# First three of eight early chunks: the current token's weights from turned keys and receptances by the tensor engine, and the weighted values added through the unit matrix

## The chip, the cores and the metric

The kernel runs on one core of one Trainium2 chip. The core has a tensor engine (PE, which writes to the accumulator memory PSUM), a vector engine (DVE), a scalar engine (ACT), a general engine (POOL) and a sync engine (SP), which here only issues transfers. The engines run their own instruction streams and meet at semaphores. The metric is device microseconds of one execution, a median of several runs; lower is better.

## What is computed

Two stages. The first is a linear recurrence over time with a bonus for the current token (4 batches, 8 heads, 768 steps, 48 numbers a head):

```python
for t in range(S):
    kt, vt, rt = (k[:, :, t], v[:, :, t], r[:, :, t])
    cur = np.einsum('bhd,bhe->bhde', u[None] * kt, vt)
    y[:, :, t] = np.einsum('bhd,bhde->bhe', rt, state + cur)
    state = w[None, :, :, None] * state + np.einsum('bhd,bhe->bhde', kt, vt)
```

The second takes y as 3072 rows of 384 numbers: `h = x @ w_in; g = h * np.cos(h); return g @ w_out`, with 2048 columns in the middle. So the current token enters y with the weight a = sum over d of r·u·k (per token and head), times v; earlier tokens enter with powers of w.

## The kernel before

The recurrence is cut into chunks of 128 tokens of one batch. The first eight (EARLY = 8; chunks 0 to 3 are the first 128 tokens of the four batches, 4 to 7 the second) go the way shown below; the rest goes in half chunks of two batches. The second stage runs in six blocks of four chunks. One unit of it, h, is nine matmuls of 512 columns (L509; high and low parts of x and of w_in), followed on DVE and ACT by the cosine and the split of g into high and low parts, and later by nine matmuls with w_out (L522). A block can begin when its four chunks have their x, so chunks 0 to 3 feed the first unit and chunks 4 to 7 the third.

An early chunk takes these steps (helper `chunk`, L956 ff.): load r, k, v (SP); turn r and k (L1001, PE) and multiply them by tables of powers of w on the way out of PSUM (rT L1010, kT L1029, or the copy L1043 when k was decayed before it was turned); multiply kT and rT into scores, A (L1093, PE); m = r·k (L1016), times u (L1050), summed over each head's 48 numbers to `a` (L1057); write `a` on the diagonal of A by eight ACT instructions of one head each (L1066) or by two wide ones (L1072); copy the scores above the diagonal over it under a mask (L1101, two per chunk, DVE); x = v times A (L1128, PE), from chunk 4 on also the state part (L1115); the state z = k times v (L1162); x in high and low parts (xh L1183, xl L1192). The weights are turned into high and low parts of another format on the way (`conv`, L884 to L925; its last step for w_in is w_in_lo, L916).

Before the chunks, w is loaded and turned (L682), raised to powers (L689 to L699) and spread into the tables decT_r and decT_k (L722, L731); u is loaded to 32 partitions (L665) and copied to the other 96 (L674).

What sets the order: every step is an `op` with an engine, a cost, what it comes after and the buffers it takes. `Plan.one_pass` goes through them and on each engine picks, among those ready within a hold, the one with the lowest due time. The due times (DUES), holds (HOLDS) and second choices of engine (ALTS) are tables of numbers, one entry per op. PE gets short matmuls of zeros (L1758) where the planner sees it idle before the second stage. Buffers are rings: three k, three v, two r, six f, four half chunks of A, seven PSUM banks for the early chunks. A buffer is loaded anew when its last reader is done.

Of the kernel before, what the change touches and what calls it, by code (L numbers as in the profile page):

```python
# [9 lines left out]
F32 = mybir.dt.float32  # L10
F32R = mybir.dt.float32r
BF16 = mybir.dt.bfloat16
I32 = mybir.dt.int32
# [24 lines left out]
RAW_K = 2  # L38
EARLY = 8

DUES = (
# [398 lines left out]
def kernel(  # L440
# [34 lines left out]
    G = 32  # L475
# [1437 lines left out]
```

## Time and profile before

| | us |
|---|---|
| median of 3 runs | 483.97 (483.74 to 484.13) |
| the profiled execution | 484.58 |
| its span, first to last instruction | 482.9 |
| PE busy in the span | 472.4 |
| DVE, ACT, POOL busy | 365.4, 297.9, 212.1 |

The span is what the trace covers; 484.58 is the same execution's own time. In the trace a matmul in 32 bits shows two records, a transposing one a single record, so 8 matmuls of the program are 16 records. A record's end is modelled, and it overlaps the next record's start by about a tenth of a microsecond; from start to start is what a group costs. In the order printed below a row is the program's instruction.

### The profile page before, as it was taken

To read this page: it belongs to the slowest core of one execution; us is meant where nothing else is said; L and a number is where in the kernel's file an instruction comes from. 1 tells how busy PE (TensorE), PEld (TensorE's weight loads), DVE (VectorE), ACT (ScalarE), POOL (GpSimd) and SP (SyncE) were. 2 spreads that over 40 slices of the span, in tenths; PEclk is the share of its full clock that TensorE was granted. 3 is DMA by queue.
4 is the path that set the end of the run, shared out by engine and by line. 5 is a ranking of instruction groups with operands and counts; after the bars stand their busy time and mean duration, and the time that the engine had idled before them with its cause. 6 is when DMAs were issued, how large, how long until landed. Compare 5 with 4: busy or idle time off the path is not lost.

```text
span 482.9 us, 11764 instructions
## 1 busy us (share of the span) xinstructions
PE 472.4 (98%) x4480; PEld 391.5 (81%) x4480; DVE 365.4 (76%) x681; ACT 297.9 (62%) x661; POOL 212.1 (44%) x215
## 2 busy tenths in 40 slices
PE   8999999999999999999999999999999999999995
PEld 7777788788888888888888888888888888899994
DVE  7999898998998886768776876775895755744453
ACT  5988897877885555466655655655655544444342
POOL 6775438445536965546735515635534600000000
PEclk9999999999999999999999999999999999999998
DMA  7883456337258636387527636636565600010001
GB/s 151 178 204 98 128 139 167 100 103 187 76 139 173 123 70 138 84 203 158 157 63 196 158 90 126 149 99 142 164 144 137 181 24 1 25 42 2 1 1 69
DMA packets 139281, 55.39 MB, mean 115 GB/s; under 512 B 122164, under 2 KB 135124, under 8 KB 139220
## 3 DMA queue, kind: packets, MB, share of 16 engines
q1 hardware_dynamic: 139012, 54.45, 46.1%
q8 instruction: 36, 0.59, 0.5%
q14 instruction: 25, 0.20, 0.1%
q10 hardware_dynamic: 208, 0.15, 0.1%
HBM read 49.86 MB, written 4.72 MB: 113 GB/s over the span
## 4 chain that ended last, share of the span: by engine, by line
PE 88%; DVE 5%; ACT 3%; issue 1%; DMA 1%; POOL 0%; ACTq 0%; DVEq 0%; POOLq 0%
PE bank L509 39%; PE bank L522 34%; PE bank L515 7%; PE bank L1400 4%; PE bank L1480 3%; ACT A L1066 1%; DVE A L1101 1%; DVE k L1021 1%; PE bank L1093 1%; DVE f L892 1%; DMA ztu<-in_u_dram 1%; DVE w_in_lo L916 1%; DVE f L530 0%; DVE a L1057 0%; PE bank L1128 0%
## 5 line engine op out<-in xcount | busy, mean ns | idle before, releaser
L527 ACT ACTIVATE qi<-bank 128x512 int32<-128x512 f32 (+1 forms) x102 | 58.1, 573 | 103.6 <-PE bank L509 98.8
L530 DVE SCALAR_TENSOR_TENSOR f<-bank,qi 128x512 f32<-128x512 f32 (+1 forms) x102 | 66.4, 655 | 66.1 <-ACT qi L527 65.4
L509 PE MATMUL bank<-xh,w_in_hi 128*128 128x512 f32 x288 | 113.2, 393 | 0.3 <-DVE gl L1610 0.3
L509 PE MATMUL bank<-xh,w_in_lo 128*128 128x512 f32 x288 | 112.7, 391 | 0.5 <-DVE w_in_lo L916 0.5
L509 PE MATMUL bank<-xl,w_in_hi 128*128 128x512 f32 x288 | 112.3, 390 | 0.0
L522 PE MATMUL bank<-gh,w_out_hi 128*128 128x512 f32 x240 | 95.8, 399 | 0.0
L522 PE MATMUL bank<-gh,w_out_lo 128*128 128x512 f32 x240 | 93.5, 390 | 0.0
L522 PE MATMUL bank<-gl,w_out_hi 128*128 128x512 f32 x240 | 93.5, 390 | 0.0
L1610 DVE TENSOR_TENSOR gl<-bank,gh 128x512 fp32r<-128x512 f32 x94 | 64.1, 682 | 14.8 <-ACT gh L1607 13.4
L1604 DVE TENSOR_TENSOR bank<-bank,f 128x512 f32<-128x512 f32 x94 | 64.8, 692 | 11.3 <-ACT f L533 11.0
L533 ACT ACTIVATE f<-f 128x512 f32<-128x512 f32 (+1 forms) x102 | 61.2, 607 | 19.5 <-DVE f L530 19.0
L1607 ACT CAST gh<-bank 128x512 fp32r<-128x512 f32 x94 | 55.0, 585 | 28.6 <-PE bank L522 25.1
L509 PEld LDWEIGHTS bank<-xh,w_in_lo 128*128 128x128 f32 x288 | 54.1, 188 | 12.9 <-DVE w_in_lo L916 1.3
L1347 POOL TENSOR_TENSOR A<-rT,decT_r 48x512 f32<-48x512 f32 x32 | 41.5, 1296 | 50.7 <-PE bank L1480 41.9
L509 PEld LDWEIGHTS bank<-xh,w_in_hi 128*128 128x128 f32 x288 | 54.0, 188 | 11.9 <-DVE gl L1610 0.7
L509 PEld LDWEIGHTS bank<-xl,w_in_hi 128*128 128x128 f32 x288 | 54.1, 188 | 10.9
L522 PEld LDWEIGHTS bank<-gh,w_out_hi 128*128 128x128 f32 x240 | 45.0, 188 | 9.9
L522 PEld LDWEIGHTS bank<-gh,w_out_lo 128*128 128x128 f32 x240 | 45.0, 188 | 9.6
L522 PEld LDWEIGHTS bank<-gl,w_out_hi 128*128 128x128 f32 x240 | 45.1, 188 | 8.9 <-DVE gl L1610 0.3
L913 POOL TENSOR_TENSOR f<-f,raw 128x384 int32<-128x384 int32 x24 | 26.1, 1086 | 37.1 <-DVE f L904 14.4
L1381 POOL TENSOR_TENSOR A<-ident,a 64x512 f32<-64x512 f32 x32 | 34.3, 1073 | 17.1 <-DVE a L1373 15.8
L1342 POOL TENSOR_TENSOR kT<-kT,decT_k 112x512 f32<-112x512 f32 x16 | 20.9, 1306 | 27.4 <-DVE kT L1327 26.2
(144 smaller groups left out, 719.1 us busy)
## 6 DMA issues: line engine op xcount, KB each, us to landing
raw<-in_moe_w_in_dram SPq DMA_DIRECT2D x32, 384.0 KB
raw<-in_moe_w_out_dram SPq DMA_DIRECT2D x32, 384.0 KB
raw<-in_k_dram SPq DMA_DIRECT2D x63, 80.0 KB
raw<-in_r_dram SPq DMA_DIRECT2D x63, 80.0 KB
out_dram<-ot SPq DMA_DIRECT2D x80, 48.0 KB
k<-in_k_dram SPq DMA_DIRECT2D x32, 96.0 KB
f<-in_r_dram SPq DMA_DIRECT2D x32, 96.0 KB
vr<-in_v_dram SPq DMA_DIRECT2D x32, 96.0 KB
```

The source lines that it names most:

```text
L509: nc.tensor.matmul(ph, a, b_, start=(i == 0), stop=(i == len(mm) - 1))
L515: nc.tensor.matmul(acc, a[:, ts], b_[:, f, :], start=(first and i == 0), stop=(last and i == 2))
L522: nc.tensor.matmul(acc, b_[:, f, n * P : (n + 1) * P], a, start=(first and i == 0), stop=(last and i == 2), skip_group_check=True)
L527: nc.scalar.activation(qi, ph, AF.Copy, scale=INV_2PI, bias=0.25)
L530: nc.vector.scalar_tensor_tensor(q, ph, INV_2PI, qi, op0=ALU.mult, op1=ALU.subtract)
L533: nc.scalar.activation(q, q, AF.Sin, scale=TWO_PI, bias=0.5 * math.pi)
L913: return lambda: eng.tensor_tensor(ai(), ai(), cn(), op=ALU.add)
L1347: nc.gpsimd.tensor_tensor(by_batch(plane(ar, j))[rows[j]], by_batch(late_t(rT))[rows[j]], late_d(decT_r)[rows[j]], op=ALU.mult)
L1381: nc.gpsimd.tensor_tensor(plane(ar, j)[side[j]], ident2[side[j], None, :].to_broadcast(to), ab()[side[j], :, None].to_broadcast(to), op=AL ...
L1604: nc.vector.tensor_tensor(g()[:, cs], ph()[:, cs], q()[:, cs], op=ALU.mult)
L1607: nc.scalar.copy(gh()[:, cs], g()[:, cs])
L1610: nc.vector.tensor_tensor(gl()[:, cs], g()[:, cs], f32(gh())[:, cs], op=ALU.subtract)
```

## The change

For chunks 0 to 2 (AT_ONCE = 3) the weight `a` is no longer computed as r·k, times u, summed over each head, on DVE and POOL. Instead kT and rT, which are turned already, are multiplied element by element (`at_once`), and PE sums over the partitions against a two-column table `uw` (u times w, one column per head of a pair; w because the tables of kT and rT together leave one power of w missing). The weights stay in PSUM. DVE multiplies v by them (`now`), and PE adds the result to x with the unit matrix as the moving operand: three matmuls behind the sixteen of x. The diagonal is not written for these chunks; A is cleared once at the start. Chunks 3 to 7 keep the old way. The small u is loaded beside w and turned with it; the broadcast u comes later, to all 128 partitions, by SP; the second u table for the late half chunks comes by four transfers of SP instead of a copy on POOL. Turning k and r is written as one helper. All three tables of numbers (DUES, HOLDS, ALTS) are replaced.

```diff
 RAW_K = 2
+AT_ONCE = 3
 DUES = (
-    -328531, -62964, -53730, -52379, -98597, -44677, 159483, 213367, -486938, 215042, 149540, 213072, 5035,
...
         def start_pool2():
             nc.gpsimd.memset(zt, 0.0)
+            nc.gpsimd.memset(A_all, 0.0)
...
-        def spread_u():
-            for n in range(1, P // G):
-                nc.scalar.copy(u_b[n * G : (n + 1) * G], u_b[0:G])
-
+        o_u = op(ACT, -199.5, 0.6, lambda: nc.scalar.dma_start(ur[:, 0:D], u), lat=0.9)
...
         def w_t():
             for j in range(2):
-                nc.tensor.matmul(b_w()[j * DP : (j + 1) * DP, 0:NP], wr, ident[0:H, j:H:2], start=True, stop=True)
+                for n, rows in enumerate((wr, ur)):
+                    nc.tensor.matmul(
+                        b_w()[j * DP : (j + 1) * DP, n * NP : (n + 1) * NP], rows, ident[0:H, j:H:2], start=True, stop=True
+                    )
...
+        def rows_u():
+            for j in range(2):
+                ps = slice(j * DP, (j + 1) * DP)
+                nc.vector.tensor_tensor(uw[ps, :, j : j + 1], b_w()[ps, NP : 2 * NP, None], pe[ps, :, 1:2], op=ALU.mult)
...
+        o_ub = op(
+            SP,
+            -1,
+            1.0,
+            lambda: nc.sync.dma_start(u_b.rearrange("p h d -> p (h d)"), u.rearrange("h d -> (h d)").partition_broadcast(P)),
+            bufs=[u_1],
+            lat=2.5,
+        )
...
-            o_u2 = op(POOL, 110, 1.9, swap_u, [last_A[0], o_u], [u_2, u_1], port=True)
+            o_u2 = op(SP, 110, 2.4, load_u, [last_A[0]], [u_2], lat=2.5)
...
+            def at_once(eng):
+                return lambda: eng.tensor_tensor(cube(mb)[0:KP], kT()[0:KP], rT()[0:KP], op=ALU.mult)
+
+            def a_of():
+                return xp()[:, NK * C : NK * C + H]
+
+            def mm_u():
+                for p in range(NP):
+                    nc.tensor.matmul(
+                        a_of()[:, 2 * p : 2 * p + 2], cube(mb)[0:KP, p, :], uw[0:KP, p, :], start=True, stop=True
+                    )
+
+            def now():
+                nc.vector.tensor_tensor(
+                    heads(vab), vb()[:, :, 0:D], a_of()[:, :, None].to_broadcast([P, H, D]), op=ALU.mult
                 )
...
+            if i < AT_ONCE:
+                o_m = op(
+                    POOL, due - 2.0, 1.35, at_once(nc.gpsimd), [e_k, e_r, o_gate], [kT, rT, mb], port=True,
+                    alts=[(DVE, 0.62, at_once(nc.vector), True)],
+                )
+                o_a = op(PE, due - 1.6, 0.5, mm_u, [o_m, o_uw], [mb, xp], lat=0.3)
+                o_d = [op(DVE, due - 1.5, 0.5, now, [o_a, l_v], [xp, vb, vab])]
...
+                for kk in range(NK if i < AT_ONCE else 0):
+                    nc.tensor.matmul(
+                        x[:, kk, :], vab()[:, kk * C : (kk + 1) * C], ident, start=False, stop=True, skip_group_check=True
+                    )
```

How the order moves, at three places. On ACT, the first instructions of the program; `wr` holds w by rows, `upper_113` the small u, `ztu` the broadcast u and the states' copies, `A` the diagonals. Before:

```order
L656 DMA wr<-in_w_dram 8x48
L665 DMA ztu<-in_u_dram 32x384
L676 ACT_TABLE_LOAD
L676 ACTIVATE tiny<-tiny 1x1
L674 COPY ztu<-ztu 32x384 x3
L731 COPY decT_k<-decT_r 128x512
L743 COPY dec_k<-bank 128x384
L1066 ACTIVATE A<-ident,a_119 128x128 x8
L1143 COPY ztu<-zc_104 48x4x48 x2
```

and now:

```order
L667 DMA upper_113<-in_u_dram 8x48
L663 DMA wr<-in_w_dram 8x48
L668 ACT_TABLE_LOAD
L668 ACTIVATE tiny<-tiny 1x1
L731 COPY decT_k<-decT_r 128x512
L743 COPY dec_k<-bank 128x384
L1177 COPY ztu<-zc_104 48x4x48
L1217 CAST xh<-bank 128x384
```

The load of w moved from first to second place, and the copies of u and the diagonals of the first chunks are gone.

On DVE, from where both tables are ready to the masks of the first chunks; `f` holds r·k before and v times its weight now, `k_77` to `k_79` are the k buffers. Before:

```order
L1010 TENSOR_TENSOR rT_84<-bank,decT_r 112x512
L1057 TENSOR_REDUCE a_119<-f_89 128x8
L1029 TENSOR_TENSOR kT_82<-bank,decT_k 112x512
L1016 TENSOR_TENSOR f_90<-vr,k_78 128x384
L1021 TENSOR_TENSOR k_78<-k_78,dec_k 128x8x48
L1205 TENSOR_TENSOR zc_104<-bank,pw 112x192
L1101 COPY_PREDICATED A<-upper,bank 128x512
L1057 TENSOR_REDUCE a_120<-f_90 128x8
```

and now:

```order
L1016 TENSOR_TENSOR rT_84<-bank,decT_r 112x512
L1016 TENSOR_TENSOR kT_81<-bank,decT_k 112x512
L1016 TENSOR_TENSOR kT_82<-bank,decT_k 112x512
L1007 TENSOR_TENSOR k_77<-k_77,dec_k 128x8x48
L1119 COPY_PREDICATED A<-upper,bank 128x512
L1059 TENSOR_TENSOR f_91<-vr,bank 128x384
L1119 COPY_PREDICATED A<-upper,bank 128x512 x2
L1007 TENSOR_TENSOR k_79<-k_79,dec_k 128x8x48
L1239 TENSOR_TENSOR zc_104<-bank,pw 112x192
```

The sums over a head gave way to products with v, the masks moved up, and two decays of k stand here on DVE.

On PE, from the first scores on; L1093 before is L1111 now (scores), L1128 is L1158 (x), L1001 is L1002 (turning), L1162 is L1196 (state). Before:

```order
L1093 MATMUL bank<-rT_84,kT_81 128x128 x8
L1162 MATMUL bank<-vr,k_77 48x48 x8
L1093 MATMUL bank<-rT_83,kT_82 128x128 x8
L1001 MATMUL bank<-ident,vr 112x128 x4
L1758 LDWEIGHTS warm
L1758 MATMUL bank<-warm 128x256
L1162 MATMUL bank<-vr,k_78 48x48 x8
```

and now:

```order
L1111 MATMUL bank<-rT_83,kT_81 128x128 x8
L1002 MATMUL bank<-ident,vr 112x128 x4
L1054 MATMUL bank<-uw,f_89 128x2 x4
L1111 MATMUL bank<-rT_84,kT_82 128x128 x8
L1196 MATMUL bank<-vr,k_77 48x48 x8
L1054 MATMUL bank<-uw,f_90 128x2 x4
L1158 MATMUL bank<-A,vr 32x128 x16
L1167 MATMUL bank<-ident,f_91 128x128 x3
```

The weights' matmuls (L1054) and the additions through the unit matrix (L1167) moved in between the scores and behind x. Further on, PE's first unit h stands behind the scores of six chunks and the x of five; before it stood behind the scores of five and the x of four.

## Rows read from the trace of the kernel before

**Rows 1.** The page: busy us by engine, share of the span, instructions.

```profile
PE 472.4 (98%) x4480; PEld 391.5 (81%) x4480; DVE 365.4 (76%) x681; ACT 297.9 (62%) x661; POOL 212.1 (44%) x215
```

**Rows 2.** Stretches: length, busy time (instructions) by engine, granted clock, DMA share, GB/s.

```profile
4.18:26.26 22.08, 20.55 (x348) 16.93 (x347) 21.02 (x40) 18.09 (x52) 16.53 (x20) 1.00 0.87 178
26.26:46.39 20.13, 18.75 (x360) 15.01 (x356) 19.53 (x39) 17.61 (x48) 12.28 (x15) 1.00 0.53 142
46.39:54.62 8.23, 7.93 (x51) 6.02 (x47) 6.20 (x14) 5.33 (x11) 3.13 (x3) 1.00 0.51 146
54.62:470.00 415.38, 415.21 (x3677) 344.87 (x3678) 313.19 (x563) 251.25 (x535) 177.14 (x161) 1.00 0.45 111
```

**Rows 3.** Timeline of the first microseconds: start, duration, engine, line, [idle before, releaser].

```profile
0.92 0.62 ACTq L656 DMA_DIRECT2D wr<-in_w_dram  x1
...
1.58 0.34 ACTq L665 DMA_DIRECT2D ztu<-in_u_dram  x1
...
2.61 0.38 PE L682 MATMUL bank<-ident,wr 8*64 8x4 f32 x4
...
4.12 1.55 ACT L674 COPY ztu<-ztu 32x384 f32<-32x384 f32 x3 [0.68 <-DMA ztu<-in_u_dram]
...
5.51 0.17 DVE L706 TENSOR_TENSOR pq<-pq 128x8 f32<-128x8 f32 x1
...
5.70 0.69 DVE L1010 TENSOR_TENSOR rT<-bank,decT_r 112x512 f32<-112x512 f32 x1
5.75 0.18 POOL L730 COPY tiny<-decT_r 1x1 f32<-1x1 f32 x1 [1.90 <-ACT ztu L674]
```

**Rows 4.** Timeline of PE alone, up to the fifth unit of the second stage.

```profile
20.00 1.16 PE L1093 MATMUL bank<-rT,kT 48*128 48x128 f32 x16
...
26.26 0.50 PE L509 MATMUL bank<-xh,w_in_hi 128*128 128x512 f32 x1
...
29.03 0.60 PE L1001 MATMUL bank<-ident,vr 128*112 128x128 f32 x4
...
40.92 0.86 PE L1115 MATMUL bank<-rT,ztu 112*32 112x128 f32 x24
41.60 1.08 PE L1128 MATMUL bank<-A,vr 128*32 128x128 f32 x32
42.61 0.56 PE L1162 MATMUL bank<-vr,k 128*48 128x48 f32 x16
...
46.39 0.50 PE L509 MATMUL bank<-xh,w_in_hi 128*128 128x512 f32 x1
...
49.33 0.69 PE L763 MATMUL bank<-ident,decT_k 128*64 128x64 f32 x16
...
54.62 0.50 PE L509 MATMUL bank<-xh,w_in_hi 128*128 128x512 f32 x1 [0.30 <-DVE gl L1610]
```

**Rows 5.** The chain in order of time: start, length, a unit h undisturbed.

```profile
58.99 2.04 PE bank L509 x9
```

**Rows 6.** DVE by line between 5.59 and 27.25 us: busy, mean ns, idle before.

```profile
L1101 DVE COPY_PREDICATED A<-upper,bank 128x512 f32<-128x512 int32 x8 | 5.8, 727 | 0.5 <-ACT A L1066 0.5
...
L1057 DVE TENSOR_REDUCE a<-f 128x8 f32<-128x384 f32 x5 | 2.7, 536 | 0.2 <-POOL f L1050 0.2
...
L1016 DVE TENSOR_TENSOR f<-vr,k 128x384 f32<-128x384 f32 x2 | 1.1, 548 | 0.0
```

**Rows 7.** Timeline: a decay of k on DVE that starts beside a POOL product.

```profile
9.96 1.00 POOL L1050 TENSOR_TENSOR f<-f,ztu 128x384 f32<-128x384 f32 x1 [0.76 <-DVE f L1016]
9.99 1.39 DVE L1021 TENSOR_TENSOR k<-k,dec_k 128x384 f32<-128x384 f32 x1
```

**Rows 8.** ACT by line from 4.18 to 46.39 us, columns as in rows 6.

```profile
L1066 ACT ACTIVATE A<-ident,a 128x128 f32<-128x128 f32 x60 | 18.5, 390 | 2.4 <-DVE a L1057 2.2
```

**Rows 9.** The page's group of a wide POOL product, columns as in rows 6.

```profile
L1342 POOL TENSOR_TENSOR kT<-kT,decT_k 112x512 f32<-112x512 f32 x16 | 20.9, 1306 | 27.4 <-DVE kT L1327 26.2
```

**Rows 10.** Waits of PE: what it waited for, us in total, times, longest.

```profile
PE bank L1093 <- ACT kT L1043: 1.5, 3, 0.5
```

More of the change, by code (lines that the diff above doesn't have):

```diff
@@ L644, in start_dve, with start_rows @@
             nc.vector.memset(pq[:, :, 8:9], 1.0)
-        o_wr = op(DVE, -100, 0.1, lambda: nc.vector.memset(wr[:, D:DP], 1.0), lat=0.1)
+        def start_rows():
+            nc.vector.memset(wr[:, D:DP], 1.0)
+            nc.vector.memset(ur[:, D:DP], 0.0)
+            nc.vector.memset(uw, 0.0)
+        o_wr = op(DVE, -100, 0.3, start_rows, lat=0.1)
         o_id = op(POOL, -100, 0.6, lambda: make_identity(nc, ident))
         o_pool = op(POOL, -99, 1.2, start_pool)
-        o_pool2 = op(POOL, -98, 1.5, start_pool2)
+        o_pool2 = op(POOL, -98, 3.3, start_pool2)
         o_dve = op(DVE, -99, 0.3, start_dve)
@@ L1036, in chunk @@
-            early_kd.append(o_kd)
-            if not first:
-                t_k = op(PE, due - 2.5, 0.49, tr(kTp, kb), [o_kd, o_pool], [kb, kTp, kT], lat=0.3)
-                e_k = op(
-                    ACT,
-                    due - 2.3,
-                    0.5,
-                    lambda: nc.scalar.copy(kT()[0:KP], cube(kTp)[0:KP]),
-                    [t_k],
-                    [kTp, kT],
-                    alts=[(DVE, 0.6, lambda: nc.vector.tensor_copy(kT()[0:KP], cube(kTp)[0:KP]), False)],
-                )
@@ L1049, in bonus_u, with decay @@
-            def bonus_u(eng):
-                return lambda: eng.tensor_tensor(heads(mb), heads(mb), u_b, op=ALU.mult)
-            o_mu = on(either(bonus_u, 0), due - 2.2, [o_m, o_u], [mb, u_1])
-            o_a = op(
-                DVE,
-                due - 1.6,
-                0.5,
-                lambda: nc.vector.tensor_reduce(ab(), heads(mb), op=ALU.add, axis=AX.X),
-                [o_mu],
-                [mb, ab],
-            )
+            def decay(eng, buf, dec):
+                return lambda: eng.tensor_tensor(buf()[:, :, 0:D], buf()[:, :, 0:D], dec, op=ALU.mult)
@@ new lines, in turn @@
+            def turn(dst, src, raw, table, tab_ready, dec, dec_ready, l, at, o_m=None):
+                if raw:
+                    t = op(PE, at - 2.5, 0.49, tr(src, l[1]), [l[0], o_pool], [l[1], src, dst], lat=0.3)
+                    return t, op(
+                        DVE,
+                        at - 2.3,
+                        0.62,
+                        lambda: nc.vector.tensor_tensor(dst()[0:KP], cube(src)[0:KP], table[0:KP], op=ALU.mult),
+                        [t, tab_ready],
+                        [src, dst],
+                    )
+                o = on(either(lambda eng: decay(eng, l[1], dec), 0), at - 2.7, [l[0], dec_ready, o_m], [l[1]])
+                t = op(PE, at - 2.5, 0.49, tr(src, l[1]), [o, o_pool], [l[1], src, dst], lat=0.3)
+                e = op(
+                    ACT,
+                    at - 2.3,
+                    0.5,
+                    lambda: nc.scalar.copy(dst()[0:KP], cube(src)[0:KP]),
+                    [t],
+                    [src, dst],
+                    alts=[(DVE, 0.6, lambda: nc.vector.tensor_copy(dst()[0:KP], cube(src)[0:KP]), False)],
+                )
+                return o, e
@@ new lines, in bonus, with bonus_u @@
+            def bonus(eng):
+                return lambda: eng.tensor_tensor(heads(vab), rb()[:, :, 0:D], kb()[:, :, 0:D], op=ALU.mult)
+            def bonus_u(eng):
+                return lambda: eng.tensor_tensor(heads(vab), heads(vab), u_b, op=ALU.mult)
+            o_m = on(either(bonus, 1), due - 2.8, [l_r, l_k, o_gate], [rb, kb, vab]) if i >= AT_ONCE else None
+            t_r, e_r = turn(rT, rTp, True, decT_r, o_dtr, None, None, (l_r, rb), due + 0.1)
+            o_kd, e_k = turn(kT, kTp, first, decT_k, o_dtk, dec_k, o_dk, (l_k, kb), due, o_m)
@@ new lines, in chunk @@
+            if first:
+                o_kd = on(either(lambda eng: decay(eng, kb, dec_k), 2), due + 1.0, [o_kd, o_dk, o_m], [kb])
+            early_kd.append(o_kd)
+            def at_once(eng):
[6 more added lines that the diff above has]
+                        a_of()[:, 2 * p : 2 * p + 2], cube(mb)[0:KP, p, :], uw[0:KP, p, :], start=True, stop=True
+                    )
@@ L1074, in spread_a @@
                 )
-            o_d = [
-                op(
-                    ACT,
-                    due - 1.55 + 0.01 * j,
-                    1.18,
-                    diagonal(j),
-                    [o_a, o_pool],
-                    [ab, A[j]],
-                    alts=[(POOL, 1.35, spread_a(nc.gpsimd, j), True), (DVE, 0.65, spread_a(nc.vector, j), True)],
-                )
-                for j in range(2)
-            ]
+            if i < AT_ONCE:
+                o_m = op(
+                    POOL, due - 2.0, 1.35, at_once(nc.gpsimd), [e_k, e_r, o_gate], [kT, rT, mb], port=True,
+                    alts=[(DVE, 0.62, at_once(nc.vector), True)],
+                )
+                o_a = op(PE, due - 1.6, 0.5, mm_u, [o_m, o_uw], [mb, xp], lat=0.3)
+                o_d = [op(DVE, due - 1.5, 0.5, now, [o_a, l_v], [xp, vb, vab])]
+            else:
+                o_mu = on(either(bonus_u, 0), due - 2.2, [o_m, o_ub], [vab, u_1])
+                o_a = op(
+                    DVE,
+                    due - 1.6,
+                    0.5,
+                    lambda: nc.vector.tensor_reduce(ab(), heads(vab), op=ALU.add, axis=AX.X),
+                    [o_mu],
+                    [vab, ab],
+                )
+                o_d = [
+                    op(
+                        ACT,
+                        due - 1.55 + 0.01 * j,
+                        1.18,
+                        diagonal(j),
+                        [o_a, o_pool, *masked],
+                        [ab, A[j]],
+                        alts=[(POOL, 1.35, spread_a(nc.gpsimd, j), True), (DVE, 0.65, spread_a(nc.vector, j), True)],
+                    )
+                    for j in range(2)
+                ]
             def mm_a():
@@ L1103, in mask @@
                 )
-            e_A = [op(DVE, due - 1.4 + 0.01 * j, 0.68, mask(j), [o_A, o_d[j], o_pool2], [Ap[j], A[j]]) for j in range(2)]
+            e_A = [
+                op(
+                    DVE,
+                    due - 1.4 + 0.01 * j,
+                    0.68,
+                    mask(j),
+                    [o_A, o_pool2] + ([o_d[j]] if i >= AT_ONCE else []),
+                    [Ap[j], A[j]],
+                )
+                for j in range(2)
+            ]
+            if i < AT_ONCE:
+                masked.extend(e_A)
             def xv():
```

77 lines of the change are left out of this document (20 added, 57 removed), and 347 rows, old and new, of tables (ALTS, DUES, HOLDS).

## The prediction

> **What bounds the kernel now.** I read the page first, then the stretches, then the first 55 us instruction by instruction. The page says that PE is busy for 472.4 us, 98% of the span [rows 1]. The stretches say where the rest is: from 54.62 to 470 us PE is busy for 415.21 of 415.38 us [rows 2], so that no edit of the first chunks can gain anything there, and every matmul added there would cost its whole length. Ahead of that, the kernel starts up: PE lacks 1.5 and 1.4 us in the two stretches up to 46.39, and part of what it is busy with is zeros (23 warm-up matmuls). There DVE is the full engine, 21.02 of 22.08 us and 19.53 of 20.13, while ACT is at 18.09 and 17.61 [rows 2]. So the question is at what time PE has the start-up behind it, with how much work done.
>
> Three marks on PE measure it: the first unit h at 26.26, the second at 46.39, the fifth at 54.62 [rows 4]. An undisturbed unit takes 2.04 us [rows 5].
>
> **The change part by part.** *Added on PE.* Three additions through the unit matrix per chunk. Low end: a 128x128 matmul of the scores, 8 in 1.16 us [rows 4], 0.145 each, 0.43 per chunk. High end: the sixteen narrow ones of x fill the array's 128 columns four at a time, and take 1.01 us from 41.60 to 42.61 [rows 4], 0.25 for each four, 0.76 per chunk. The added ones are 128 rows deep like those of x, so I take 0.65. Four matmuls of two columns per chunk, eight records: low end 0.35, by 16 records in 0.69 (49.33) [rows 4]; high end 0.76, by four records in 0.38 [rows 3]. I take 0.5, since the weights are 128 columns wide rather than 64. Three chunks: 3.4 us (2.3 to 4.6), all of it within the first 20 us, where PE waits for DVE anyway; uncovered it would be the whole 3.4.
>
> *The tables come later.* PE's first small matmuls (2.61) need w; the change needs w and u there, and w is now the second transfer on ACT's queue. The first was used 1.69 us after its issue (0.92, 2.61), the second 2.54 us after it (1.58, 4.12) [rows 3]. So the second is there between 3.27 and 4.12; I take 3.5, nearer to the small one, since the second of before was 48 KB. That is 0.9 later. Two more small matmuls add 0.2, two small DVE products ahead of the table (each like the 0.17 of L706 [rows 3]) 0.3. The first rT goes from 5.70 to 7.1.
>
> Of the Trainium skill one rule speaks to this: "DMA: Bandwidth & Descriptors", section "Queues, rings and completion order", has each of the 16 DMA engines take turns between queues, a packet from each. By that rule w would wait for a packet of SP's first load alone and be nearer to 3.3; the late use at 4.12 agrees with it as far as it goes, as the engine was held by at least one load. It is a rival below.
>
> *DVE up to the first unit.* Between 5.59 and 27.25 us (the end of w_in_lo) DVE runs 36 instructions (masks, sums and products among them in [rows 6]). In the new order 43 stand there. More: two masks (0.65 each from start to start; the record is 0.73 [rows 6]), one rT and one `at_once` (0.6 each), one addition of states (0.28), one decay of k (0.7 to 1.39 [rows 7]) and three products `now` at 0.5, priced by the product of 0.55 [rows 6], since the operand from PSUM is broadcast but as long. Less: two sums, 0.46 each [rows 6]. Together +4.4. Without any wait saved, w_in_lo would end at 27.25 + 1.4 + 4.4 = 33.05. The waits of before in that stretch are 0.5 for a diagonal, 0.2 for POOL [rows 6] and about as much again in gaps that have no named cause. Followed instruction by instruction with these durations, the order ends w_in_lo at 31.5, and PE, which now has the x of a fifth chunk ahead of the unit, begins h at 31.9.
>
> *What of that is only moved.* Ahead of h PE now has two turnings more (0.5 each, by the 0.60 record less its overlap), one set of scores (1.1) and one x with state (0.68 and 1.01 from 40.92 to 42.61) [rows 4]: 3.8 us. The even point is 26.26 + 3.8 = 30.06. At 31.9 the new kernel is 1.8 behind, half of the added PE work being hidden.
>
> *From the first unit to the second.* Before, h took from 26.26 to 29.03, 2.77 for 2.04 of work: 0.73 of waiting for w_in_lo. From 29.03 to 46.39 PE has five turnings, three scores, three states (0.5), four x with state and six matmuls of 0.227, 15.4 us in 17.36: 1.9 of waits, and of these 0.9 are for the copy of kT on ACT (two of the three waits of 0.5 in [rows 10]). In the new order w_in_lo is there when h begins, and the ACT engine has 24 diagonal pieces less, 24/60 of 18.5 us, 7.4 [rows 8]. I follow the order to 1.1 us of waits for the same section (one, of 0.9, for kT of chunk 6, since two other copies and a cosine stand before it on ACT). So 1.8 - 0.73 - 0.8 = 0.3 behind at the second unit.
>
> *From the second to the fifth.* Before, 8.23 us [rows 2] for three units, three output matmuls (0.69) and the late table (0.62): 7.43. The 0.8 that are left are waits, the last of them for gl at 54.62 [rows 4]. The new order has the late table before, the three units in a row, and gl 0.1 us ahead of need: -0.7. Sum: 0.3 - 0.7 = -0.4 at the fifth unit, and PE is full from there, so it stays to the end.
>
> *Costed at nothing.* Clearing A (2048 columns) on POOL, some 2 us, lies in its 1.90 us of waiting [rows 3]; if not, the first masks are late by the difference. The broadcast u on SP (192 KB at 178 GB/s [rows 2], 1.1 us) pushes the second k by that, which is needed only after the late tables; uncovered 1.1. The four late transfers of u stand on SP ahead of weight loads whose buffers are not free then. POOL: two `at_once` of 1.3 [rows 9] for two products and three products with u of 1.0; it is not full. Taken away besides: the copies of u on ACT, 1.55 [rows 3], off the path once the tables are late.
>
> **The sum.** The profiled execution took 484.58, 0.61 above the median of 483.97. 484.58 - 0.4 = 484.2; in the terms of the median 483.6. A difference of 0.2%, 0.97 us, is about what a measurement of this kernel can tell from none, so this is no change.
>
> **The rivals.** *Slower: DVE waits for POOL.* A decay of k on DVE took 1.39 us [rows 7] where the product of the same size took 0.55 [rows 6]: it started 30 ns after a POOL product and lasted until that ended. In the new start-up six DVE instructions are of that kind (three decays, two products of r and k, one `at_once`), with two inputs from SBUF, and POOL has 16 products to put beside them; I have counted two such waits. "SBUF — State Buffer", section "Who interferes with whom", of the Trainium skill has this as a lock on one port pair, for the whole instruction, whoever comes first; the row agrees. Each further wait is up to 0.85. From two more on, with the wait for h behind, the new kernel is above 484.9; at three, 483.6 + 2.1 = 485.7 with what they delay on ACT. For it: DVE is at 95% already, and the order adds to it. Against: DVE has 2.0 us free from 46.39 to 54.62 [rows 2].
>
> *Faster: the tables are hardly later.* If w lands as it did, 1.69 after its issue, or in the turn of the queues, the first rT is at 6.3 and all that follows moves up by 0.8: 482.8. For it: few bytes. Against: the small transfer of before was issued ahead of all loads but one, and u, behind them, took 2.54.
>
> *Faster: ACT was the brake.* The waits of PE for kT are all on ACT [rows 10], and the diagonals wait 2.2 us for sums [rows 8]; both chains are cut for the first three chunks. If the 0.9 wait that I kept goes, and DVE's gaps with it (0.6), 483.6 - 1.5 = 482.1. Against: ACT's load is not the highest.
>
> **How the numbers follow.** Forecast 483.6, band 483.0 to 484.9: 0.40. Slower by the lock: 0.26. Faster by ACT: 0.21; by early tables: 0.13. The range that leaves about one in ten on either side runs from 481.9 (both gains, less a part) to 485.6 (three locks); the bounds of PE's added work (-1.1, +1.2) are hidden behind DVE by half and lie inside. Faster 0.34, same 0.40, slower 0.26.
>
> **What would show it.** In the changed profile: PE's first small matmuls at 3.3 to 3.6; first unit near 31.9, second near 47.3, fifth near 54.2; the additions at 0.22 each; no diagonal before chunk 3; DVE above 95% up to 46 us; decays of k on DVE above 1 us no more than twice. Wrong if PE has waits over 0.5 us after 55 us (a weight that comes late in the new order), if the first unit is before 30.5 or after 33, or if the added matmuls stand where PE was full.

## The result, and the profile after

The changed kernel takes 487.71 us (median of 6 runs, 485.87 to 488.47) against 483.75 us before (6 runs beside them): ratio 1.0075, 95% interval 1.0052 to 1.0097. It is slower by some 4 us where I forecast no change, and lies above the range that I gave. A second set of runs, beside the experiments, gave 1.0060 (1.0046 to 1.0074). The profiled execution took 488.16 us with a span of 486.4, so 3.6 us more than the one of before.

The loss stands ahead of the fifth unit h, which starts at 59.55 instead of 54.62 [rows 4]; from there to the end of the span the changed kernel is 1.4 us shorter (0.7 of it up to PE's last matmul, 0.6 behind it). First the page's busy times (columns as in [rows 1]): PE has 6.0 us and 48 matmul records more, ACT 9.4 us less (mostly the diagonals of three chunks and the copies of u), DVE 1.1 less.

```profile
PE 478.4 (98%) x4528; PEld 399.3 (82%) x4528; DVE 364.3 (75%) x685; ACT 288.5 (59%) x630; POOL 212.2 (44%) x215
```

Next the stretches of the start-up (columns as in [rows 2]), the same 19 us of the kernel before and then of the changed one:

```profile
8.00:27.00 19.00, 17.69 (x322) 14.05 (x322) 18.07 (x32) 16.25 (x49) 15.04 (x16) 1.00 0.82 170
```

```profile
8.00:27.00 19.00, 19.00 (x257) 16.94 (x259) 13.63 (x26) 4.89 (x13) 9.32 (x12) 0.91 0.64 135
...
14.00:16.00 2.00, 2.00 (x40) 1.91 (x42) 2.00 (x5) 0.35 (x1) 0.34 (x1) 0.91 0.37 71
16.00:19.00 3.00, 3.00 (x34) 2.62 (x25) 1.21 (x3) 0.09 (x1) 0.00 (x0) 0.50 0.95 236
```

These rows hold the result. Before, DVE was full (18.07 of 19.00) and PE had gaps. Now PE is busy for all of the stretch, DVE falls to 13.63, ACT from 16.25 to 4.89, POOL from 15.04 to 9.32: the full engine has changed. And the granted clock, 1.00 in this stretch before, is 0.50 (1.2 GHz of 2.4) from 16 to 19 us, though PE shows no idle time from 3.90 on.

The timeline of PE in the changed kernel (columns as in [rows 4]):

```profile
3.90 0.40 PE L674 MATMUL bank<-ident,wr 8*64 8x4 f32 x3 [0.60 <-DMA wr<-in_w_dram]
...
6.66 1.06 PE L1002 MATMUL bank<-ident,vr 128*112 128x128 f32 x4
7.52 0.84 PE L1792 MATMUL bank<-warm 128*128 128x256 bf16 x3
8.16 0.92 PE L1002 MATMUL bank<-ident,k 128*112 128x128 f32 x4
8.92 0.49 PE L1792 MATMUL bank<-warm 128*128 128x256 bf16 x3
...
10.43 1.16 PE L1111 MATMUL bank<-rT,kT 48*128 48x128 f32 x16
...
12.01 0.95 PE L1054 MATMUL bank<-uw,f 112*128 112x2 f32 x8
...
14.48 1.05 PE L1054 MATMUL bank<-uw,f 112*128 112x2 f32 x8
15.46 1.83 PE L1158 MATMUL bank<-A,vr 128*32 128x128 f32 x32
17.22 1.65 PE L1167 MATMUL bank<-ident,f 128*128 128x128 f32 x6
...
20.32 1.10 PE L1158 MATMUL bank<-A,vr 128*32 128x128 f32 x32
21.36 0.94 PE L1167 MATMUL bank<-ident,f 128*128 128x128 f32 x6
...
37.56 0.50 PE L507 MATMUL bank<-xh,w_in_hi 128*128 128x512 f32 x1
...
52.61 0.50 PE L507 MATMUL bank<-xh,w_in_hi 128*128 128x512 f32 x1
...
59.55 0.42 PE L507 MATMUL bank<-xh,w_in_hi 128*128 128x512 f32 x1
```

What to see: PE waits 0.60 for w, and its small matmuls start at 3.90 (2.61 before [rows 3]). Three warm matmuls take 0.84 at 7.52 and 0.49 at 8.92, so PE runs at half its speed until then. (The trace's records of the granted clock begin at 8.81 us, at 1.00; the 1.00 that the columns of a stretch give for the time ahead of that is no reading. The expectations below count the full clock from there, and from 5.2 in the kernel before.) Two turns stand 1.50 apart (6.66, 8.16). The first scores (L1111) start at 10.43. L1054 are the two-column matmuls, L1167 the additions. The x of the first chunk takes 1.83 and its additions 1.65, at 0.50 of the clock; the same two groups of the second chunk take 1.10 and 0.94. First h at 37.56, second at 52.61, fifth at 59.55.

And DVE (columns as before), which now waits for PE:

```profile
7.60 1.29 DVE L1016 TENSOR_TENSOR rT<-bank,decT_r 112x512 f32<-112x512 f32 x2
...
13.00 0.56 DVE L1059 TENSOR_TENSOR f<-vr,bank 128x384 f32<-128x384 f32 x1 [0.57 <-PE bank L1054]
...
23.11 0.55 DVE L1059 TENSOR_TENSOR f<-vr,bank 128x384 f32<-128x384 f32 x1 [0.92 <-PE bank L1054]
```

### The profile page after: what moved, and what is told of

It is laid out like the page before. It is cut to its first block, busy times and chain, and to the rows that moved or that the text cites. A ratio compares the mean times of both kernels' runs of the same rounds, so it can differ in the third digit from the quotient of the medians.

```text
span 486.4 us, 11853 instructions
## 1 busy us (share of the span) xinstructions
PE 478.4 (98%) x4528; PEld 399.3 (82%) x4528; DVE 364.3 (75%) x685; ACT 288.5 (59%) x630; POOL 212.2 (44%) x215
## 4 chain that ended last, share of the span: by engine, by line
PE 96%; DVE 1%; ACT 1%; DMA 0%; ACTq 0%; issue 0%
PE bank L507 40%; PE bank L520 35%; PE bank L513 7%; PE bank L1434 4%; PE bank L1514 3%; PE bank L1111 2%; PE bank L1002 1%; PE bank L1158 1%; PE bank L1196 1%; PE bank L1167 1%; PE bank L1792 1%; PE bank L1054 1%; ACT A L1067 1%; DMA wr<-in_w_dram 0%; PE bank L1145 0%; DVE k L1007 0%
## 5 line engine op out<-in xcount | busy, mean ns | idle before, releaser
L923 POOL TENSOR_TENSOR f<-f,raw 128x384 int32<-128x384 int32 x25 | 26.9, 1077 | 37.4 <-DVE f L914 15.4
```

Source lines behind the costliest of these rows:

```text
L923: return lambda: eng.tensor_tensor(ai(), ai(), cn(), op=ALU.add)
```

## The theories

H, the head: w lands late, so the tables and the first scores are late, and PE stays slow for longer. P, the added matmuls: PE is full from the first scores on, so each of them costs its length. C, the clock: its half stretch. O, the new order and its waits by themselves make it slower. All experiments keep the order of the instructions that remain; differences in us are of medians, against the runs of the kernel before on the same chip.

## Experiments on the late w

**The kernel before with u first and w second** (`before_w_second`):

```diff
         o_w = op(
-            lambda: nc.scalar.dma_start(wr[:, 0:D], w),
+            lambda: nc.scalar.dma_start(
+                u_b.rearrange("p h d -> p (h d)")[0:G], u.rearrange("h d -> (h d)").partition_broadcast(G)
+            ),
...
         o_u0 = op(
-            lambda: nc.scalar.dma_start(
-                u_b.rearrange("p h d -> p (h d)")[0:G], u.rearrange("h d -> (h d)").partition_broadcast(G)
-            ),
+            lambda: nc.scalar.dma_start(wr[:, 0:D], w),
```

> The kernel before with its two small loads on ACT's queue exchanged: u's 16 rows first, w second, as the changed kernel has them. Nothing else moves. Theory H (the late head: w lands about 1.3 us later, the tables with it, and PE's granted clock rises later): the first small matmuls start at 3.6 to 3.9 instead of 2.61, decT_r at 6.2 to 6.8 instead of 4.90, the granted clock is full only some 2 to 3.5 us later than 5.2, the first h comes 1 to 2.5 us after 26.26, and the time is 484.8 to 486.3. Theory P (the time comes from PE matmuls that were added, nothing from the head): the walk had slack ahead of the first A, the first h comes within 0.5 of 26.26 and the time is 483.4 to 484.2.

Measured: 485.28 us (10 runs) against 483.80, ratio 1.0028 (1.0015 to 1.0040), +1.5 us. Its PE timeline:

```profile
3.87 0.38 PE L682 MATMUL bank<-ident,wr 8*64 8x4 f32 x4 [1.19 <-DMA wr<-in_w_dram]
...
8.42 1.06 PE L1001 MATMUL bank<-ident,vr 128*112 128x128 f32 x4
9.27 1.01 PE L739 MATMUL bank<-ident,decT_k 128*128 128x128 f32 x4
10.12 0.60 PE L1001 MATMUL bank<-ident,k 128*112 128x128 f32 x4
10.76 1.16 PE L1093 MATMUL bank<-rT,kT 48*128 48x128 f32 x16
...
28.41 0.50 PE L509 MATMUL bank<-xh,w_in_hi 128*128 128x512 f32 x1
```

As H said. w is there at 3.87, 1.26 us later, and the first scores start at 10.76, 2.6 us after the 8.12 of before. (The load ahead of w is that of u to 32 partitions here, a small one of 8x48 in the changed kernel; w is used at nearly the same time, 3.87 and 3.90.) A turn takes 1.06 until about 9 and 0.60 at 10.12. Of the 2.6 us, 2.15 are left at the first h (26.26 before) and 2.2 at the end of this profile, which is one of the slowest of the ten runs; by the medians it is 1.5.

**The changed kernel with w first** (`after_w_first`):

```diff
         o_w = op(
-            lambda: nc.scalar.dma_start(wr[:, 0:D], w),
+            lambda: nc.scalar.dma_start(ur[:, 0:D], u),
...
-        o_u = op(ACT, -199.5, 0.6, lambda: nc.scalar.dma_start(ur[:, 0:D], u), lat=0.9)
+        o_u = op(ACT, -199.5, 0.6, lambda: nc.scalar.dma_start(wr[:, 0:D], w), lat=0.9)
...
         def w_t():
             for j in range(2):
-                for n, rows in enumerate((wr, ur)):
-                    nc.tensor.matmul(
-                        b_w()[j * DP : (j + 1) * DP, n * NP : (n + 1) * NP], rows, ident[0:H, j:H:2], start=True, stop=True
-                    )
+                nc.tensor.matmul(b_w()[j * DP : (j + 1) * DP, 0:NP], wr, ident[0:H, j:H:2], start=True, stop=True)
```

The matmuls of ur, to another bank, stand behind those of `tab_t`, and `rows_u` behind the first turned k; six warm matmuls stand ahead of and behind `w_t` instead of nine and three.

> The changed kernel with w's load first and u's second on ACT's queue, only w's small matmuls ahead of the powers, u's small matmuls behind the turn of the decays, the rows of u made on DVE behind the first turned k, and six warm matmuls ahead of and six behind w's small ones, as before. All work stays. Theory H: small matmuls at 2.6 to 2.9, decT_r near 5.0, full clock by 5.5 and no half-clock stretch at 15.6 to 19.1, fifth h 1.5 to 3 us earlier than 59.55, time 484.7 to 486.3. Theory P: fifth h within 0.5 of 59.55 and the time within 0.6 of the changed kernel's, since PE has the same matmuls to do.

Measured: 485.87 us (5 runs) against 483.80, ratio 1.0044 (1.0026 to 1.0063), +2.1 us.

```profile
2.66 0.38 PE L673 MATMUL bank<-ident,wr 8*64 8x4 f32 x4
...
9.03 1.16 PE L1120 MATMUL bank<-rT,kT 48*128 48x128 f32 x16
...
34.57 0.50 PE L507 MATMUL bank<-xh,w_in_hi 128*128 128x512 f32 x1
```

The first scores are at 9.03 instead of 10.43, and the first h is 3.0 us earlier than in the changed kernel, 1.4 of it by the start and 1.6 by the clock, which stayed full in this execution. By the medians over the kernel before it is 1.0 to 1.9 us faster than the changed kernel; the intervals overlap, so the marks show this gain and the times alone don't. More than half of the loss is still there: H is a part.

## Experiments on the added matmuls

**Without the added work** (`after_no_new`): at_once, mm_u, now and the loop of additions do nothing, so the current token is missing from the first three chunks.

```diff
             def at_once(eng):
-                return lambda: eng.tensor_tensor(cube(mb)[0:KP], kT()[0:KP], rT()[0:KP], op=ALU.mult)
+                return lambda: None
...
-                for kk in range(NK if i < AT_ONCE else 0):
+                for kk in range(0):
```

> The changed kernel in its order without the added work: for the first three chunks the products of turned k and r, the two-column matmuls, v times the weights and the three additions through the unit matrix are left out, so that the current token is missing from these chunks; the diagonal of A is left out there too, as in the changed kernel. The late head stays. Theory P: each chunk gives back 1.65 us of PE (0.88 + 0.77) and the stretch at half clock goes with them (about 1.5), so the fifth h comes 5 to 6.5 us earlier than 59.55, at 53 to 54.5, and the time is 481.5 to 483. Theory H: PE waits again for DVE and the tables, at most 2.5 us come back, and the time is 485 to 486.5. Theory O (the new order alone, by its waits and buffers): less than 1 us comes back, time over 486.8.

Measured: 482.10 us (10 runs) against 483.80, ratio 0.9973 (0.9960 to 0.9986), -1.7 us. The first scores start about as in the changed kernel:

```profile
10.53 1.16 PE L1106 MATMUL bank<-rT,kT 48*128 48x128 f32 x16
...
31.22 0.50 PE L507 MATMUL bank<-xh,w_in_hi 128*128 128x512 f32 x1
```

The first h is 6.3 us earlier than in the changed kernel. Where the clock stays full on both sides, the way from the first scores to the first h is 4.85 us shorter (20.69 against the 25.54 of `after_again` below). P holds, and O does not: with the late w still in it, but without the added work, the new order is faster than the kernel before.

**Each kind by itself**: without the two-column matmuls (`after_no_mm_u`, the diff), and without the additions (`after_no_add`, the last two lines of the diff above).

```diff
             def mm_u():
-                for p in range(NP):
-                    nc.tensor.matmul(
-                        a_of()[:, 2 * p : 2 * p + 2], cube(mb)[0:KP, p, :], uw[0:KP, p, :], start=True, stop=True
-                    )
+                pass
...
-                    heads(vab), vb()[:, :, 0:D], a_of()[:, :, None].to_broadcast([P, H, D]), op=ALU.mult
+                    heads(vab), vb()[:, :, 0:D], dec_k, op=ALU.mult
```

> The changed kernel without the two-column matmuls of the first three chunks: v is multiplied by the table dec_k in SBUF instead of their result, so the current token has wrong weights there; the products on POOL and DVE, v's multiplication and the three additions stay. If PE is full from the first A on: 3 x 0.88 = 2.6 us come back, 485.1 from 487.7. If these matmuls are also what the granted clock falls behind (they end just before it falls at 15.63): no half-clock stretch either, another 1.5, 483.5. If PE is not what binds: under 1 us, above 486.7.

> The changed kernel without the three additions through the unit matrix of each of the first three chunks; all else of the added work stays, the two-column matmuls too, and the current token is missing from x there. If PE is full: 3 x 0.77 = 2.3 us come back, and the half-clock stretch behind the two-column matmuls stays, of which 0.65 us fell on an addition: 484.5 to 485.5. If the clock stays full here too: 483.5 to 484.2. If PE does not bind: above 486.7.

Measured: 484.39 us without the two-column matmuls (ratio 1.0010, 0.9999 to 1.0020, +0.8) and 484.77 without the additions (1.0019, 1.0004 to 1.0035, +1.2); 10 runs each, against 483.62. So either kind is worth 2 to 3 us, about what PE spends on it: the two-column ones 0.88 per chunk from start to start, the additions 0.77. Half-clock stretches: none in the profile of the first, one in that of the second:

```profile
16.00:19.00 3.00, 3.00 (x34) 2.40 (x25) 1.90 (x4) 1.07 (x3) 0.11 (x1) 0.50 1.03 245
```

**The added work on PE alone** (`after_pe_only`), against a lock or a wait on DVE and POOL; `at_once` and `now` do nothing:

```diff
-                        a_of()[:, 2 * p : 2 * p + 2], cube(mb)[0:KP, p, :], uw[0:KP, p, :], start=True, stop=True
+                        a_of()[:, 2 * p : 2 * p + 2], kT()[0:KP, p, :], uw[0:KP, p, :], start=True, stop=True
...
-                        x[:, kk, :], vab()[:, kk * C : (kk + 1) * C], ident, start=False, stop=True, skip_group_check=True
+                        x[:, kk, :], vb().rearrange("q h d -> q (h d)")[:, kk * C : (kk + 1) * C], ident, start=False, stop=True, skip_group_check=True
```

> The changed kernel with the added work of PE alone: the two-column matmuls read turned k instead of the products, the additions read v instead of v times the weights, and the products on POOL and DVE and v's multiplication on DVE are left out for the first three chunks; the current token is wrong there. If PE is full and what the added work costs is PE's own: within 0.6 of the changed kernel. If DVE, POOL, their shared port or the wait of the two-column matmuls for the products binds: 1 to 3 us below it.

Measured: 487.38 us (4 runs) against 483.49, ratio 1.0068 (1.0046 to 1.0090), where the changed kernel itself, beside it, has 486.53 (1.0060). That is 0.85 above it, a little outside the 0.6 that I expected, and not below it. Its profile has the half stretch too and can be set beside the changed kernel's first one:

```profile
10.41 1.16 PE L1109 MATMUL bank<-rT,kT 48*128 48x128 f32 x16
...
37.55 0.50 PE L507 MATMUL bank<-xh,w_in_hi 128*128 128x512 f32 x1
```

From the first scores to the first h it takes 27.14 us, there 27.13 (10.43 to 37.56). Taking away all that DVE and POOL were given brings nothing back. What the added work costs is PE's own.

Why do matmuls of two columns take so long? The profile's weight loads (PEld) answer, from 8 to 40 us of the changed kernel, and beside them the matmuls of the same line:

```profile
L1054 PEld LDWEIGHTS bank<-uw,f 112*128 112x128 f32 x24 | 2.9, 191 | 0.1
```

```profile
L1054 PE MATMUL bank<-uw,f 112*128 112x2 f32 x24 | 3.0, 245 | 0.0
```

The loads of their weights (128 columns each) fill 2.9 of the 3.0 us. The Trainium skill has the rule: "TensorE: Matmul & The Clock Gate", section "LDWEIGHTS (loading the stationary operand)", lets a weight load cost by its columns alone; by its formula a load of 128 takes 107 ns, an estimate, and a chunk's eight records 0.85 us. The trace agrees: 0.88 was measured for the first and third chunk, 0.98 for the second.

## Experiments on the clock

**12 warm matmuls instead of 9 ahead of the small ones** (`after_more_warm`), so that PE is busy while w is on its way:

```diff
-                    n = int(min(o.gap, 6.0) / 0.22) if started is None else int(o.gap / 0.35)
+                    n = int(min(o.gap, 6.0) / 0.22) + 3 * (o is o_wT) if started is None else int(o.gap / 0.35)
```

> The changed kernel with 12 warm matmuls instead of 9 ahead of the small ones, so that PE does not stand idle at 3.30 to 3.90 until w has landed. The result is the same. Theory H with the clock as its larger part: the granted clock is full 1.5 to 3.5 us earlier than 8.81, the turns at 5.17, 6.66 and 8.16 take 0.6 instead of 1.06 each, and the time falls by 0.5 to 1.5, to 486.2 to 487.2. If only the landing counts (the tables set the pace) or only the added matmuls: the clock may rise earlier but the first A stays within 0.3 of 10.43 and the time within 0.4 of the changed kernel's.

Measured: 489.73 us (4 runs) against 483.80, ratio 1.0118 (1.0101 to 1.0135), +5.9: 2 to 3 us slower than the changed kernel, where I expected a gain. PE's timeline and the stretches:

```profile
4.65 0.60 PE L1002 MATMUL bank<-ident,vr 128*112 128x128 f32 x4
...
5.42 0.60 PE L1002 MATMUL bank<-ident,vr 128*112 128x128 f32 x4
...
9.19 1.16 PE L1111 MATMUL bank<-rT,kT 48*128 48x128 f32 x16
...
11.53 1.05 PE L1054 MATMUL bank<-uw,f 112*128 112x2 f32 x8 [0.59 <-POOL f L1047]
...
14.10 1.66 PE L1054 MATMUL bank<-uw,f 112*128 112x2 f32 x8
15.69 1.94 PE L1158 MATMUL bank<-A,vr 128*32 128x128 f32 x32
```

```profile
14.00:16.00 2.00, 2.00 (x24) 1.92 (x20) 1.94 (x5) 0.35 (x1) 0.34 (x1) 0.59 0.32 58
16.00:19.00 3.00, 3.00 (x38) 2.53 (x31) 0.99 (x2) 0.00 (x0) 0.00 (x0) 0.50 0.89 219
19.00:21.00 2.00, 2.00 (x13) 1.66 (x14) 0.78 (x2) 1.06 (x2) 0.00 (x0) 0.50 0.02 7
```

The half that was expected came true: with no gap ahead of the small matmuls the first turn takes 0.60 at once and the next stands 0.77 behind it, and the first scores start at 9.19, 1.2 us earlier. But the clock then falls during the second chunk's two-column matmuls and stays at 0.50 for over 6 us. (PE has gaps here up to 11.53, none from there to the fall.)

**The same without the two-column matmuls** (`more_warm_no_mm_u`, both edits above):

> The kernel with 12 warm matmuls ahead of the small ones, whose half-clock stretch was the longest, without the two-column matmuls (v is multiplied by the table dec_k instead; wrong weights of the current token in the first three chunks). If the granted clock falls behind the two-column matmuls: it stays full, the first A is at 9.1 to 9.4 instead of 10.77, and the time is 482.6 to 483.6. If it falls because PE ran warm matmuls without a break from the start: a half-clock stretch again between 13 and 21, and the time is 485 to 487.

Measured: 483.81 us (10 runs) against 483.49, ratio 1.0003 (0.9993 to 1.0013). The same stretches:

```profile
14.00:16.00 2.00, 2.00 (x22) 1.70 (x22) 2.00 (x4) 0.93 (x3) 1.18 (x2) 1.00 0.84 165
16.00:19.00 3.00, 2.95 (x59) 2.31 (x59) 3.00 (x7) 0.50 (x2) 0.82 (x2) 1.00 0.89 218
```

The clock stays at 1.00, in the profile and, by the means of the ten runs (0.997 and more), in all; with the two-column matmuls it fell in four of four. The warm matmuls are not what it falls behind. The time is 0.2 above the range that I expected.

**Warm matmuls in the place of the two-column ones** (`after_u_as_warm`):

```diff
             def mm_u():
-                for p in range(NP):
-                    nc.tensor.matmul(
-                        a_of()[:, 2 * p : 2 * p + 2], cube(mb)[0:KP, p, :], uw[0:KP, p, :], start=True, stop=True
-                    )
+                warm_up(4)
```

> As the run without the two-column matmuls, but with four warm matmuls of 128x256 in the place of each chunk's, 4 x 0.22 = 0.88 us on PE, the same length. The weights of the current token are wrong there. If the fall of the granted clock comes behind the kind of matmul (few columns between weight loads): the clock stays full, and the time is 1.5 below the changed kernel's, about 486.2, and 2.6 above the run without them. If it comes from the filled PE as such, or from what ran before: the half-clock stretch is there again and the time is 487 to 488.

Measured: 485.65 us (10 runs) against 483.62, ratio 1.0033 (1.0022 to 1.0044), clock 1.00 in the profile. The length was misjudged: four warm matmuls take 0.53 from start to start at PE's full speed, not 0.88. Against the run without anything there it costs 1.3 us, near the 3 x 0.53 of PE's time. PE is as full as in the changed kernel:

```profile
8.00:27.00 19.00, 19.00 (x299) 16.10 (x298) 16.79 (x31) 6.84 (x18) 11.19 (x12) 1.00 0.78 163
```

So a full PE alone does not bring the clock down. That the two-column matmuls do, in some executions, rests on the pair of runs above and on the count below.

**The changed kernel again** (`after_again`, no edit):

> The changed kernel itself, unchanged, beside the next three on one chip, so that they have its time there: 486 to 488.5. If the half-clock stretch of its profile is part of its usual time and not of that one execution, its runs fall into a group near 488 and one near 486, with the lower mean granted clock at the longer times.

Measured: 486.53 us (5 runs, 486.00 to 487.27), ratio 1.0060. The two groups did not come here: all five have a mean granted clock of 0.998 or 0.999, and the profiled one, 487.27 us, has no half stretch:

```profile
14.00:16.00 2.00, 2.00 (x38) 1.82 (x34) 2.00 (x5) 0.00 (x0) 0.43 (x1) 1.00 0.50 95
```

```profile
10.53 0.60 PE L1002 MATMUL bank<-ident,k 128*112 128x128 f32 x4
11.06 1.16 PE L1111 MATMUL bank<-rT,kT 48*128 48x128 f32 x16
...
16.09 1.10 PE L1158 MATMUL bank<-A,vr 128*32 128x128 f32 x32
17.13 0.94 PE L1167 MATMUL bank<-ident,f 128*128 128x128 f32 x6
...
36.60 0.50 PE L507 MATMUL bank<-xh,w_in_hi 128*128 128x512 f32 x1
```

Here PE is slow for longer (the first scores at 11.06) but the x and the additions take 1.10 and 0.94. From the first scores to the first h: 25.54 us, against 27.13 in the first profile. So the half stretch costs 1.6 us where it comes as in the first profile, and the loss of about 3 us is there without it. The two groups came in other kernels: `after_w_first_lean` below has four runs of 485.32 to 485.55 with a mean granted clock of 0.993 and six of 483.70 to 484.60 with 0.997 or more, 1.2 us between their medians. Over all executions, the mean granted clock is 0.995 or lower in 14 of the 44 of changed kernels with the two-column matmuls (2 of 11 of the changed kernel itself, 4 of 4 with more warm matmuls), and in none of the 44 of changed kernels without them, nor in any of the kernel before. The 14 are the least: every profile shows 0.50 at the end of its span too, so that a mean of 0.996 stands both for the profile of `after_no_add`, with a half stretch, and for that of `before_w_second`, without one.

## Both parts taken out, and the best version found

**w first, and without the added work** (`w_first_no_new`, the edits of after_w_first and after_no_new):

> Both at once: w's load first with u's small matmuls behind the turn of the decays, and without the added work (the current token is missing from the first three chunks). If the late head and the added matmuls add up: 482.1 less 1.5 to 1.8, 480.2 to 480.8. If the head is hidden once the added matmuls are gone (PE waits for DVE again): 481.6 to 482.3.

Measured: 481.18 us (4 runs) against 483.49, ratio 0.9949 (0.9932 to 0.9965), -2.3 us. Between the two expectations: without the added matmuls the late w costs 0.6 by the medians (the intervals touch) rather than 1.5 to 1.8, and PE has gaps again (18.23 busy of the 19.00 us from 8). This is what the new order and the work removed are worth together, by themselves.

**w first and a lean head** (`after_w_first_lean`): no warm matmuls between the early turns, and the broadcast of u for later chunks is SP's ninth load instead of its fourth (the expectation counts it as the eighth). The diff is against the kernel with w first:

```diff
-                    n, heads_6 = (6, heads_6 - 1) if heads_6 else (n, 0)
+                    n, heads_6 = (6, heads_6 - 1) if heads_6 else (n if started else 0, 0)
...
+            def load_v():
+                load(vb, v)()
+                if i == 1:
+                    nc.sync.dma_start(u_b.rearrange("p h d -> p (h d)"), u.rearrange("h d -> (h d)").partition_broadcast(P))
```

> The changed kernel with w first and the small matmuls of u behind the turn of the decays, and two more edits in the head: no warm matmuls between the early turns (11 fewer), and the broadcast of u for the later chunks is the eighth load on SP's queue instead of the fourth, behind v of the second chunk. The result is the same. If PE is full from the first A on, each us by which the first A is earlier counts: k of the second chunk lands 0.7 us earlier and the first A starts at 7.3 to 8.3 instead of 9.03, time 484.2 to 485.3. If the granted clock falls without the warm matmuls, or the turns stay slow: 485.5 to 487.5. If the loads set the pace again behind the first A: the time of the run with w first, 485.9.

Measured: 484.58 us (10 runs) against 483.62, ratio 1.0020 (1.0008 to 1.0033). First scores at 8.37, as expected from a full PE: 0.66 earlier than with w first alone, the first h 0.66 earlier too. Which of the two edits gives this was not separated. It is the best version that computes everything, and still 1.0 us slower than the kernel before (0.7 by its six runs with the higher mean clock); no version that computes everything beat the kernel before.

## Why the prediction was wrong, point by point

- **The bound.** That DVE is "the full engine" and PE lacks 1.5 us up to the first h was read rightly, but of the kernel before. Of each of three chunks the change takes two products, a sum and eight diagonal pieces from DVE, POOL and ACT, gives back two products, and gives PE matmuls, and I kept DVE as the bound for the new order. In the 19 us from 8 on DVE has 13.63 and PE 19.00; forecast above 95% up to 46 us, DVE is at 82% from 4.18 on.
- **The step that failed** is "all of it within the first 20 us, where PE waits for DVE anyway". PE's whole lack there was 22.08 - 20.55 = 1.5 us [rows 2]; 3.4 us, by my own sum, had no room in it. I never added up PE's own path: the even point 30.06, the added 3.4 and the 1.4 by which the tables are late, less at most 1.5 of waits, give 33.4, later than the 31.9 by DVE's path. The condition that I named as the case in which I would be wrong, "if the added matmuls stand where PE was full", is what happened: `after_no_new` against the changed kernel, 4.7 to 5.7 us.
- **The prices.** Two-column matmuls 0.5 per chunk, measured 0.88, above my high end of 0.76: I priced columns of output, where the loads of 128 weight columns count. The bounds, 16 records in 0.69 and four in 0.38, came from matmuls with 64 weight columns, and the one reason that I gave for going up from the low end, the 128 columns, was the term itself. Additions 0.65, measured 0.77, the high end. Together 4.95 us for three chunks instead of 3.4.
- **The head.** w at 3.5, measured 3.90 (the 1.69 that I took for the first load is only a bound, as PE was busy with zeros up to 2.61); first rT at 7.1, measured 7.60. Not priced at all was that PE, idle ahead of the small matmuls, stays slow until 8.9: two turns with three warm matmuls between them stand 1.50 apart instead of 0.77 (`after_more_warm`). First scores: 10.43, against 8.12 before.
- **The clock** was not thought of: 1.6 us in the profiled execution.
- **The sum at the first h.** Even point 30.06, measured 37.56: added matmuls 4.95, first scores later 2.3, half clock 1.6, less 1.4. That is 7.5; I had 1.8. The 1.4 is the remainder; the rows of PE between the first scores and the first h show 2.05 us of waits and zeros before and 0.84 now, 1.2 of it.
- **What held.** From the first unit to the second I forecast 15.4 us (31.9 to 47.3), measured 15.05; from the second to the fifth 6.9 (47.3 to 54.2), measured 6.94. So behind the first unit the sum holds within 0.4 us. PE has no wait after 55 us. Decays of k on DVE above 1 us: one (1.37 at 37.42), so the lock of which "SBUF — State Buffer", section "Who interferes with whom", of the Trainium skill tells has no part in the loss; `after_pe_only` says the same. (The decay of [rows 7] did not end with the POOL product, as I read it, but 0.4 us behind it, at 11.38 against 10.96.)
- **The rivals for a gain.** The rival by ACT is not shown: PE's waits for kT went only from 1.5 us (three) to 1.0 (two). What `w_first_no_new` shows is that order and relief of DVE, POOL and ACT together are worth 2.3 us, where this rival had 1.9; the added matmuls take twice that. The early tables did not come; w was 0.4 later than forecast, not 0.2 earlier.

In us over the kernel before: order and relief -2.3, late w +0.6, added work +4.7 to +5.7 (the half clock in some executions among it), sum +3.0 to +4.0. Taken away in the other sequence the split is another: late w +1.0 to +1.9 (`after_w_first`), added work +4.4 (`after_w_first` against `w_first_no_new`). With the added matmuls PE is full and a late start counts more; the larger part is theirs either way.

## What to carry to other kernels

When a change moves work from a full engine to one with gaps, set the work given against the gaps of the taker (its length less its busy time in that stretch) before anything is called hidden. Price a matmul by the longer of its columns and its weight load; for the two-column ones here it was the load. A load that is moved to second place on its queue delays all that waits for it (w by 1.3 us here), and where PE stood idle for it, slow matmuls lasted longer behind it.

## What was not expected of the hardware

- Matmuls of two columns with 128 weight columns cost 0.11 to 0.12 us a record (0.88 to 0.98 for eight); weight loads fill 2.9 of 3.0 us.
- The granted clock fell to half (1.2 GHz) behind such matmuls while PE had no idle time for several us: from about 15.6 to 19 us in the first profile (PE busy from 3.90 on), from 14 to 21 with more warm matmuls (busy from 11.53 on). "TensorE: Matmul & The Clock Gate", section "HAM oscillation — how this bites in real kernels", of the Trainium skill ties a loss of clock to gaps in PE's work; these rows show one without a gap. That it came in at least 14 of 44 executions with these matmuls and in none of 44 without is measured; why in some and not in others is open.
- At the start, matmuls take twice their time (a turn 1.06, later 0.60) up to the trace's first record of the granted clock. In the six profiles in which PE is busy up to the small matmuls this ended between 4.1 and 7.5 us (4.1 and 6.0 with 12 warm matmuls), in the seven with a gap of 0.5 to 0.6 ahead of them between 8.5 and 10.1, with one of 1.19 at 10.1. So one and the same head can differ by more than 1 us between executions (8.81 and 10.1 in the two profiles of the changed kernel).
- What a late w costs the changed kernel is shown by marks (1.4 us at the first scores); the times of the two kernels overlap.
